# Batch 1's loads in another order: v from SyncE behind a VectorE write, weights and q, k ahead of the weighing on GpSimd

## The chip, the core and the metric

The kernel runs on one core of a Trainium2 chip. The time is the device time of one execution in microseconds (us), and the median of several executions counts. The profile is of one execution; its span runs from the first to the last instruction, and all positions below are microseconds from the span's start.

## What is computed

Attention with a forget gate over 8 batches of 8 heads (576 tokens, head size 64), and then a two-layer feed-forward with an exact gelu over the 4608 tokens of width 512 (hidden width 2048):

```
scores = q @ k.T / 8
cum    = cumsum(log(clip(f, 1e-4, 1)), axis=-1)
scores = where(causal, -1e9, scores + cum[:, :, :, None] - cum[:, :, None, :])
attn   = softmax(scores)
x      = (attn @ v) laid out as [batch * tokens, heads * 64]
h      = x @ w_in
out    = (0.5 * h * (1 + erf(h / sqrt(2)))) @ w_out
```

All inputs and the output are float32 in memory.

## The kernel before, in words

The gate never enters the scores. The kernel computes a running product of f (`wT`, per token and head) and multiplies v by it: row j of v, and an extra column of ones, are scaled ("weighed") by token j's factor into the bf16 tile `vw`. Attention is then exp(scores) times `vw`, divided by the extra column. `weigh_v` (lines 283 to 295) does this for two heads at a time, on GpSimd for all batches but a part of batch 0: one product of 128x640 (line 288) and one cast of the factors (line 295). `vw` has one buffer and `v_sb`, the float32 tile that v is loaded into, has one too; so batch 1's v cannot be loaded before batch 0's last weighing (line 764) has read it.

Tokens lie on the 128 partitions in five blocks (the last overlaps the fourth and uses 64 partitions). Of a batch, two heads form a pair; for each pair TensorE computes four tiles of scores (line 319), ScalarE takes the exponential (line 329), GpSimd masks the diagonals (line 331), TensorE multiplies by `vw` (`attend`, line 350), and VectorE divides (lines 363, 364). The result is transposed into `xT`, and the feed-forward follows: `gemm1` (line 405), gelu on ScalarE (line 425), `gemm2` in several forms (lines 449, 509, 545, 569).

The schedule is written by hand: the order of the program text is the order of each engine's queue, and an engine that waits holds up all that is queued behind it. Work of neighbouring batches is interleaved on TensorE, so that the feed-forward of batch b fills the gaps of the attention of batch b+1.

Batches 0 and 1 have q and k loaded into stacked tiles (`load_qk_tokens`, lines 98 to 125): the tile called "q" holds q and k of heads 0 to 3, the tile called "k" those of heads 4 to 7, so a row of the profile that reads `k<-in_k_dram` is k of heads 4 to 7. TensorE transposes them, a pair of heads at a time (`transposes_first`, lines 217 to 241, matmuls of line 226). From batch 2 on, SyncE (SP) transposes q and k by DMA (line 255), and VectorE sorts them (line 269).

Transfers that convert float32 to bf16 are issued from GpSimd: q and k, w_in in quarters (line 184), w_out in quarters of 512 rows (line 188). v is not converted. `load_v` (lines 129 to 137) issues five transfers, one for each block of tokens, of the heads it is given, on the engine it is given, SP if none is named. Batches 0 and 1 have v issued from GpSimd, the later ones from SP.

Around the change, the parts of the text are these:

- `first_attention` (line 706) is batch 0's attention. At its lines 756 to 774 GpSimd's queue gets, in this order: w_in's quarters 0 to 2 between the weighings of batch 0, q and k of batch 1 of heads 0 to 3 (two heads at a time), the last weighing (line 764), a small write to `v_sb` (line 770), v of batch 1 for heads 0 to 3, w_in's quarter 3, q and k of heads 4 to 7 in one piece, v for heads 4 to 7.
- The loop of lines 952 to 981 is the rest of `gemm1` of a batch. At its step 7 of batch 0 (lines 965 to 972) GpSimd gets the weighing of pair 0 of batch 1, a quarter of w_out, the weighing of pair 1, another quarter of w_out, and q and k of batch 2; TensorE gets the transposes of pair 0 of batch 1.
- `second_attention` (line 882) is batch 1's attention. Its order on TensorE: the scores of pair 0 (`tiles(0, 0)`, `tiles(0, 2)`) between the transposes of pairs 1 and 2 and the held blocks 10 to 12 of batch 0's `gemm1`, the first scores of pair 1, block 13, and then `run(0)`, which is `attend` of pair 0 and is the first to read batch 1's `vw`. Blocks 12 to 15 read w_in's last quarter. The other weighings (pairs 2 and 3) and the masks of pairs 1 to 3 lie on GpSimd behind the two of step 7, in the order in which TensorE needs them. SP gets batch 2's transposes (lines 925, 926), GpSimd a small read of batch 2's k as a gate (line 931, instruction of line 595) and w_out's other half behind it.

Of the kernel before, what the change touches and what calls it, by code (L numbers as in the profile page):

```python
# [54 lines left out]
def kernel(  # L55
# [10 lines left out]
    nc = tc.nc  # L66
# [31 lines left out]
    def load_qk_tokens(b, h0=0, h1=H):  # L98

        if b >= B:  # L100
            return
        stacked = b < 2
        if b not in qk_of:
            qk_of[b] = [
                qk_pool.tile(
                    [P, H // 2, J0 * D] if stacked else [PT, H, JT * D],
                    BF16,
                    tag=n,
                    name=f"{n}{b}",
                )  # L110
                for n in "qk"
            ]
        for which, src in enumerate((q, k)):
            if stacked:
                half, g0 = divmod(h0, H // 2)
                g1 = h1 - half * (H // 2)
                dst = qk_of[b][half][which * D : (which + 1) * D, g0:g1, :]
            else:
                dst = qk_of[b][which][:, h0:h1, :]
            nc.gpsimd.dma_start(  # L120
                dst,
                src[b, h0:h1].rearrange(
                    "h (p j) d -> p h (j d)", j=J0 if stacked else JT
                ),
            )
# [3 lines left out]
    def load_v(b, h0=0, h1=H, eng=nc.sync, ns=range(NBLK)):  # L129
        if b >= B:  # L130
            return
        for n in ns:
            p0 = D if n == NBLK - 1 else 0
            eng.dma_start(  # L134
                v_sb[p0:P, h0:h1, n, :],
                v[b, h0:h1, K0[n] + p0 : K0[n] + P].rearrange("h p d -> p h d"),
            )
# [79 lines left out]
    def transposes_first(b, i, pool, tag, both=(0, 1), parts=1):  # L217

        half, g = divmod(2 * i, H // 2)
        src = qk_of[b][half]  # L220
        pss = {w: pool.tile([P, J0, D], BF16, tag=tag, name="ps_f") for w in both}
        for j in range(J0):
            for which in both:
                rows = slice(which * D, (which + 1) * D)
                for h in range(2):
                    nc.tensor.transpose(
                        pss[which][h * D : (h + 1) * D, j, :],
                        src[rows, g + h, j * D : (j + 1) * D],
                        ident_bf[rows, rows],
                    )  # L230

        for which in both:
            dst = (qT, kT)[which][i].rearrange("d (p j) -> d p j", j=J0)
            ps = pss[which].rearrange("d j p -> d p j")
            copies = [nc.vector.tensor_copy] * parts
            if b == i == 0:
                copies = [nc.vector.tensor_copy, nc.scalar.copy]
            n = D // len(copies)
            for at, copy in enumerate(copies):
                part = slice(at * n, (at + 1) * n)  # L240
                copy(dst[:, part], ps[:, part])
# [41 lines left out]
    def weigh_v(b, i, eng=nc.gpsimd, n0=0, n1=NBLK):  # L283

        hs = slice(2 * i, 2 * i + 2)
        bh = b * H + 2 * i
        w = wT[:, n0:n1, bh : bh + 2].rearrange("p n h -> p h n")
        eng.tensor_tensor(  # L288
            vw(b)[:, hs, n0:n1, 0:D],
            v_sb[:, hs, n0:n1, :],  # L290
            w.unsqueeze(3).to_broadcast([P, 2, n1 - n0, D]),
            Alu.mult,
        )
        if b:
            eng.tensor_copy(vw(b)[:, hs, :, D], w)
# [410 lines left out]
    def first_attention():  # L706

        most = NBLK - 1

        def transposes(i, which, parts=1):  # L710
            transposes_first(0, i, m_psum, "m", (which,), parts)

        warm_up(9)
        for which in range(2):
            transposes_first(0, 0, o_psum, "o", (which,))
        nc.vector.tensor_tensor_scan(
            decay[:, S - 2 :: -1],
            f_sb[:, S - 1 : 0 : -1],
            none[:, 0 : S - 1],
            2.0**80,  # L720
            Alu.mult,
            Alu.add,
        )
        warm_up(2, 2 * P)
        scores_a(0)
        scores_b(0)
        transposes(1, 0)
        transposes(1, 1, 2)
        psw = o_psum.tile([P, NBLK, BH], FP32, tag="o", name="psw")
        for n in range(NBLK):  # L730
            nc.tensor.transpose(
                psw[:, n, :], decay[:, K0[n] : K0[n] + P], ident_fp[:BH, :BH]
            )
        idle = o_psum.tile([P, TC], FP32, tag="o", name="ps_w")

        def keep():
            nc.tensor.matmul(idle, warm[:, 0:P], warm, start=True, stop=True)

        scores_a(1)
        nc.vector.tensor_copy(wT[:, 0:4, :], psw[:, 0:4, :])  # L740
        nc.vector.tensor_copy(wT[D:P, 4, :], psw[D:P, 4, :])
        nc.vector.tensor_copy(
            vw(0)[:, :, :, D], wT[:, :, 0:H].rearrange("p n h -> p h n")
        )
        transposes(2, 0)
        scores_b(1)
        transposes(2, 1)
        scores_c(0, 1)
        transposes(3, 0)
        scores_a(2)  # L750
        transposes(3, 1)
        keep()
        scores_b(2)
        weigh_v(0, 0, nc.vector, 0, most)
        weigh_v(0, 1, nc.vector, 0, most)
        load_w_in(0)
        load_v(0, 0, 8, nc.gpsimd, [most])
        load_w_in(1)
        weigh_v(0, 2, n1=most)
        weigh_v(0, 3, n1=most)  # L760
        load_w_in(2)
        load_qk_tokens(1, 0, 2)
        load_qk_tokens(1, 2, 4)
        nc.gpsimd.tensor_tensor(
            vw(0)[:, :, most, 0:D],
            v_sb[:, :, most, :],
            wT[:, most, 0:H].unsqueeze(2).to_broadcast([P, H, D]),
            Alu.mult,
        )
        nc.gpsimd.memset(v_sb[:, :, 0, 0:1], 0.0)  # L770
        load_v(1, 0, 4, nc.gpsimd)
        load_w_in(3)
        load_qk_tokens(1, 4, 8)
        load_v(1, 4, 8, nc.gpsimd)
        scores_a(3)
        keep()
        attend_0(0, 0)
        attend_0(0, 1)
        scores_c(2, 3)
        scores_b(3)  # L780
        attend_0(1, 0)
        attend_0(1, 1)
        to_xT_0(0, nc.scalar.copy)
        attend_0(2, 0)
        to_xT_0(1, nc.scalar.copy)
        attend_0(2, 1)
        scores_t(0)
        scores_t(2)
        attend_0(3, 0)
        to_xT_0(2, nc.vector.tensor_copy)  # L790
        attend_0(3, 1)

        three = range(HP - 1)
        pss = [gemm1(0, 0, three)]
        scores_t4()
        pss += [gemm1(0, 1, three, spare())]
        to_xT_0(3, nc.vector.tensor_copy)
        pss += [gemm1(0, 2, three, spare())]
        for ffb in range(3):
            gemm1(0, ffb, (HP - 1,), pss[ffb])  # L800
        gemm1(0, 3)
# [143 lines left out]
    for b in range(B):  # L945
        if b == 0:
            first_attention()
        elif b == 1:
            second_attention()
        else:  # L950
            attention(b)
        for ffb in range(4 if b < 2 else 5, n_ff):
            if b == 0 and ffb in HELD:
                continue
            aside = ffb in (7, 8) if b > 1 else b == 1 and ffb % 4 < 2
            gemm1(b, ffb, ps=spare() if aside else None)
            if b == 1 and ffb % 2 == 0:
                at = HELD[(ffb - 4) // 2]
                gelu(0, at, h_of[at])
            if b == 0:  # L960
                if ffb == 4:
                    attend_tail()
                if ffb == 5:
                    tail_0()
                if ffb == 7:
                    weigh_v(1, 0)
                    load_w_out(0)
                    weigh_v(1, 1)
                    load_w_out(1)
                    load_qk_tokens(2)  # L970
                if ffb == 7:
                    transposes_first(1, 0, o_psum, "o")
            elif b + 1 < B:
                first, gap = (5, 3) if b == 1 else (1, 4)
                at, late = divmod(ffb - first, gap)
                if late == 0:
                    untangle(b + 1, at)
                if late == gap - 2 and (b > 1 or at < 2):
                    weigh_v(b + 1, at)
                if ffb == (9 if b == 1 else 14):  # L980
                    load_qk_tokens(b + 2)
# [34 lines left out]
```

## Time and profile before

| | |
|---|---|
| median of 3 runs | 334.8 us |
| lowest, highest | 334.04, 337.23 us |
| the profiled execution's own time | 335.03 us |
| its span | 333.1 us |
| granted TensorE clock, mean | 0.999 |
| DMA packets | 94980, 44.18 MB, mean 133 GB/s |

The span is shorter than the execution's time, which also holds what lies around the instructions. In the profile PE is TensorE, PEld its weight loads, DVE is VectorE, ACT ScalarE, POOL GpSimd, SP SyncE; L350 is line 350. A row of a timeline gives start and length in us, the engine, the line, the operation, the tile written and the tiles read, shapes, the count, and in brackets the idle time of that engine just before and what ended it. DMA queue q0 carries what GpSimd issues, q1 what SP issues; a row of a queue gives packets, megabytes, and the time of the packets as a share of 16 engines' time in that stretch (packets overlap within an engine, so it can pass 100%).

In the stretch from 7 to 50 us the DMA engines are nearly always busy, at some 200 GB/s.

### The profile page before, as it was taken

The numbers are of one execution on the slowest core, as the hardware profiler recorded it, in microseconds if no ns is written. First come the engines' busy times: TensorE is split into PE (matmuls) and PEld (weight loads), VectorE is DVE, ScalarE is ACT, GpSimd is POOL, SyncE is SP. The second block draws the span as 40 slices with busy tenths as digits, with TensorE's granted clock in tenths as the row PEclk, the third lists the DMA queues.
The fourth block names the chain that finished last, engine by engine and source line by source line (L and its number), as shares of the span: only waits on it lengthen the run. The fifth ranks groups of instructions, "written<-read, shape, count | busy, mean of one in ns | idle before, by whom it ended". The sixth has DMA issues, their size and how long they took to land.

```text
span 333.1 us, 8058 instructions
## 1 busy us (share of the span) xinstructions
PE 324.5 (97%) x3287; PEld 169.5 (51%) x3287; DVE 184.3 (55%) x427; ACT 205.8 (62%) x296; POOL 135.4 (41%) x262
## 2 busy tenths in 40 slices
PE   7999799999999999999999999999999999999995
PEld 3765455445554466445644565455544654444443
DVE  6853556664549764894589447954795450010011
ACT  4886686974526786578737892788278836405600
POOL 8997873048337044704471344434432410000000
PEclk9999999999999999999999999999999999999999
DMA  7999999979999799489939896879700420020022
GB/s 122 195 193 195 214 195 146 184 150 180 203 199 175 119 213 159 96 138 184 202 106 140 169 194 130 124 146 212 155 0 3 100 76 33 0 92 36 0 51 76
DMA packets 94980, 44.18 MB, mean 133 GB/s; under 512 B 74208, under 2 KB 89824, under 8 KB 94944
## 3 DMA queue, kind: packets, MB, share of 16 engines
q1 hardware_dynamic: 77760, 27.16, 41.4%
q0 software_dynamic: 16784, 15.99, 30.5%
q8 instruction: 25, 0.41, 0.5%
q10 hardware_dynamic: 400, 0.52, 0.4%
q14 instruction: 11, 0.09, 0.1%
HBM read 36.85 MB, written 9.44 MB: 139 GB/s over the span
## 4 chain that ended last, share of the span: by engine, by line
PE 87%; POOL 6%; DMA 5%; issue 0%; ACT 0%; DVE 0%; POOLq 0%
PE ps L405 34%; PE ps L509 27%; PE ps L449 8%; PE o L350 8%; PE s L319 6%; DMA w_in_sb<-in_moe_w_in_dram 3%; DMA k<-in_k_dram 3%; POOL v_sb L169 2%; PE ps L569 1%; POOL k L120 1%; PE ps L545 1%; POOL q L120 1%; POOL vw L288 1%; POOL v_sb L134 1%; POOL w_in_sb L184 1%
## 5 line engine op out<-in xcount | busy, mean ns | idle before, releaser
L425 ACT ACTIVATE g<-ps 128x512 bf16<-128x512 f32 x138 | 78.5, 602 | 79.4 <-PE ps L405 78.8
L405 PE MATMUL ps<-xT,w_in_sb 128*128 128x512 bf16 x512 | 114.0, 379 | 0.1
L509 PE MATMUL ps<-w_out_sb,g 64*128 64x512 bf16 (+1 forms) x711 | 108.1, 377 | 0.0
L329 ACT ACTIVATE e<-s 128x896 bf16<-128x896 f32 x112 | 87.6, 836 | 22.2 <-PE s L319 19.7
L405 PEld LDWEIGHTS <-w_in_sb 128*128 128x128 bf16 x576 | 55.3, 98 | 66.5 <-issue 2.6
L331 POOL TENSOR_SCALAR_AFFINE_SELECT e<-e 128x256 bf16<-128x256 bf16 (+1 forms) x135 | 49.1, 383 | 88.6 <-ACT e L329 88.2
L509 PEld LDWEIGHTS <-g 64*128 64x128 bf16 (+1 forms) x711 | 39.4, 95 | 34.7 <-issue 4.2
L288 POOL TENSOR_TENSOR vw<-v_sb,wT 128x640 bf16<-128x640 f32 (+1 forms) x30 | 38.4, 1279 | 25.5 <-DMA v_sb<-in_v_dram 15.4
L269 DVE COPY kT<-tk 64x288 bf16<-64x288 bf16 x96 | 42.9, 447 | 2.6 <-DMA tk<-k 1.0
L269 DVE COPY qT<-tq 64x288 bf16<-64x288 bf16 x96 | 39.9, 415 | 4.0 <-DMA tq<-q 2.6
L517 DVE COPY ot<-ps 128x512 f32<-128x512 f32 x20 | 13.8, 692 | 46.9 <-PE ps L509 46.9
L319 PE MATMUL s<-qT,kT 64*128 64x256 bf16 (+1 forms) x336 | 37.1, 276 | 0.5 <-ACT e L329 0.4
L350 PEld LDWEIGHTS <-e 128*128 128x128 bf16 x840 | 30.3, 98 | 7.9 <-POOL e L331 2.5
L458 DVE COPY ot<-ps 128x512 f32<-128x512 f32 (+2 forms) x9 | 5.7, 633 | 49.6 <-PE ps L449 49.6
L350 PE MATMUL o<-vw,e 128*128 128x65 bf16 x840 | 32.3, 194 | 0.0
L364 DVE TENSOR_TENSOR x<-o,r 128x320 bf16<-128x320 f32 x56 | 27.5, 492 | 3.2 <-DMA xT<-x 1.3
L449 PE MATMUL ps<-w_out_sb,g 128*128 128x512 bf16 (+2 forms) x144 | 28.0, 355 | 0.0
L319 PEld LDWEIGHTS <-kT 64*128 64x128 bf16 x336 | 16.8, 94 | 19.2 <-issue 4.5
L449 PEld LDWEIGHTS <-g 128*128 128x128 bf16 x144 | 13.5, 98 | 14.5
L529 DVE TENSOR_TENSOR ot<-ot,ps 128x512 f32<-128x512 f32 x22 | 15.1, 685 | 1.1
L363 DVE RECIPROCAL r<-o 128x5 f32<-128x5 f32 x56 | 10.5, 188 | 9.1 <-PE o L350 9.1
L405 PE MATMUL ps<-tails,w_in_sb 128*128 128x512 bf16 x64 | 14.3, 377 | 0.0
(89 smaller groups left out, 187.9 us busy)
## 6 DMA issues: line engine op xcount, KB each, us to landing
out_dram<-ot SPq DMA_DIRECT2D x32, 256.0 KB, 2.4
v_sb<-in_v_dram SPq DMA_DIRECT2D x24, 256.0 KB, 4.8
q<-in_q_dram POOLq DMA_DIRECT2D x6, 576.0 KB, 6.5
k<-in_k_dram POOLq DMA_DIRECT2D x6, 576.0 KB, 8.7
v_sb<-in_v_dram POOLq DMA_DIRECT2D x17, 128.0 KB, 5.3
w_in_sb<-in_moe_w_in_dram POOLq DMA_DIRECT2D x4, 512.0 KB, 7.0
w_out_sb<-in_moe_w_out_dram POOLq DMA_DIRECT2D x4, 512.0 KB, 8.2
v_sb<-in_v_dram SPq DMA_DIRECT2D x6, 128.0 KB, 4.6
```

Source lines behind the costliest of these rows:

```text
L269: nc.vector.tensor_copy(rows[:, odd], src[odd * D : (odd + 1) * D, 2 * i + h].rearrange("d j p -> d p j"),)
L288: eng.tensor_tensor(vw(b)[:, hs, n0:n1, 0:D], v_sb[:, hs, n0:n1, :], w.unsqueeze(3).to_broadcast([P, 2, n1 - n0, D]), Alu.mult,)
L319: nc.tensor.matmul(to, *ab, start=half < 0, stop=half == 1 or not masked)
L329: nc.scalar.activation(et[:, :, z:c], st[:, :, z:c], Act.Exp, scale=scale)
L331: nc.gpsimd.affine_select(out=et[:, :, c0 + z : c0 + P], in_=et[:, :, c0 + z : c0 + P], compare_op=Alu.is_ge, fill=0.0, base=z, pattern=[[ ...
L350: nc.tensor.matmul(o[:, m, :], e_of[b, i, t][:, h, c : c + P], vw_of[b][:, 2 * i + h, n, :], start=(n == 0), stop=(n == m),)
L364: nc.vector.tensor_tensor(x_of[b, i][:, :, h, :], o[:, :, 0:D], r.unsqueeze(2).to_broadcast([P, NBLK, D]), Alu.mult,)
L405: nc.tensor.matmul(ps, w_in_sb[:, kt, ffb * P : (ffb + 1) * P], src[:, kt, 0:TC], start=(kt == 0), stop=(kt == n_dm - 1),)
L425: nc.scalar.activation(g_of[c][ffb], ps, Act.Gelu)
L449: nc.tensor.matmul(pss[ts][:, c0:c1], g_of[c][kt][:, ts * P : (ts + 1) * P], w_out_sb[:, kt, c0:c1], start=(kt == 0), stop=(kt == n_ff - 1),)
L509: nc.tensor.matmul(banks[r], g_of[c][kt][rows, ts * P : (ts + 1) * P], w_out_sb[rows, kt, :], start=kt == (steps.index("r") if r else 0), ...
L529: nc.vector.tensor_tensor(ot, ot, bank, Alu.add)
```

## The change

```diff
@@ first_attention
-        nc.gpsimd.memset(v_sb[:, :, 0, 0:1], 0.0)
-        load_v(1, 0, 4, nc.gpsimd)
         load_w_in(3)
-        load_qk_tokens(1, 4, 8)
-        load_v(1, 4, 8, nc.gpsimd)
+        load_qk_tokens(1, 4, 6)
+        load_qk_tokens(1, 6, 8)
         scores_a(3)
@@ the loop over gemm1, batch 0
                 if ffb == 7:
-                    weigh_v(1, 0)
+                    transposes_first(1, 0, o_psum, "o")
+                    nc.vector.memset(v_sb[:, :, 0, 0:1], 0.0)
+                    load_v(1, 0, 4)
+                    load_v(1, 4, 8)
                     load_w_out(0)
-                    weigh_v(1, 1)
                     load_w_out(1)
                     load_qk_tokens(2)
-                if ffb == 7:
-                    transposes_first(1, 0, o_psum, "o")
+                    weigh_v(1, 0)
+                    weigh_v(1, 1)
```

Batch 1's ten transfers of v are issued from SP, in place of GpSimd. The small write to `v_sb`, which the first of them waits for, is VectorE's, in place of GpSimd's, and stands on VectorE behind the copies of the transposes of pair 0. On GpSimd, w_in's last quarter and q and k of heads 4 to 7, now two heads at a time, come directly behind the last weighing of batch 0; then follow half of w_out and q and k of batch 2, and only then the weighing of pairs 0 and 1, which were between these before. On SP, v stands ahead of the transposes of batch 2. TensorE's, ScalarE's and (but for the write) VectorE's instructions and their order stay as they are.

## The prediction, made before the changed kernel was run

> **What bounds the kernel now.** I read the page's engine shares first, then the chain that ended last around the change (17 to 41 us), then the timelines of TensorE and GpSimd there, then the DMA rows of single stretches, because the change moves transfers and nothing else.
>
> ```profile
> PE 324.5 (97%) x3287; PEld 169.5 (51%) x3287; DVE 184.3 (55%) x427; ACT 205.8 (62%) x296; POOL 135.4 (41%) x262
> ```
>
> TensorE is the bound: of the 333.1 us span it is idle for 8.6. Of these, 1.3 lie before its first matmul and 4.1 after its last one (which ends at 329.08), so some 3.2 us are all that any change of order can win. The chain shows the largest piece of them:
>
> ```profile
> 17.54 9.08 DMA w_in_sb<-in_moe_w_in_dram
> 26.90 1.37 POOL v_sb L134 x2
> 28.27 0.75 POOL w_in_sb L184
> 29.64 8.40 DMA k<-in_k_dram
> 38.08 0.47 PE ps_f L226 x34
> ```
>
> Read it upwards: TensorE's transposes of heads 4 and 5 (L226) start at 38.08 because k of heads 4 to 7 (the tile "k") landed at 38.04; it was issued at 29.64 because GpSimd had stood still until w_in's third quarter landed at 26.62. In the timelines (start, length, instruction, idle time before it) TensorE loses 1.35 us there, and the first weighted attention of batch 1 (L350) follows at 39.82:
>
> ```profile
> 38.08 0.47 PE L226 MATMUL ps_f<-key_of,k 64*64 64x64 bf16 x34 [1.35 <-DMA k<-in_k_dram]
> 39.82 1.11 PE L350 MATMUL o<-vw,e 128*128 128x65 bf16 x30
> ```
> ```profile
> 20.68 1.12 POOL L764 TENSOR_TENSOR vw<-v_sb,wT 128x512 bf16<-128x512 f32 x1
> 22.14 2.32 POOL L134 DMA_DIRECT2D v_sb<-in_v_dram  x3 [0.30 <-POOL v_sb L770]
> 26.90 1.37 POOL L134 DMA_DIRECT2D v_sb<-in_v_dram  x2 [2.43 <-DMA w_in_sb<-in_moe_w_in_dram]
> 29.64 0.63 POOL L120 DMA_DIRECT2D k<-in_k_dram  x1
> 33.87 1.33 POOL L288 TENSOR_TENSOR vw<-v_sb,wT 128x640 bf16<-128x640 f32 x1
> 35.10 0.27 POOL L295 CAST vw<-wT 128x10 bf16<-128x10 f32 x1
> ```
>
> GpSimd's queue holds eight transfers: w_in, four of q and k and three of v went out from 17.54 on, and the ninth waited for the first. The weighing of heads 0 and 1 ends at 35.37, so today vw is 4.45 us early for L350. The DMA rows of five stretches carry the rest: 60 to 62 us, where GpSimd's w_out (q0) and SP's transposes (q1) run together; w_out alone (40 to 42); q and k of batch 2 alone (45 to 48); v from SP alone (64 to 66); v from GpSimd (28 to 29):
>
> ```profile
> q0 software_dynamic: 304, 0.31, 91.2%
> q1 hardware_dynamic: 306, 0.08, 29.6%
> ```
> ```profile
> q0 software_dynamic: 390, 0.38, 121.3%
> ```
> ```profile
> q0 software_dynamic: 780, 0.59, 128.5%
> ```
> ```profile
> q1 hardware_dynamic: 2019, 0.50, 129.4%
> ```
> ```profile
> q0 software_dynamic: 85, 0.21, 89.7%
> ```
>
> Each line gives packets and MB. Together the two queues take turns one packet for one packet (304 to 306), though q0's packets have 1024 bytes and q1's 256. From SP, v goes in packets of 250 bytes (0.50 MB in 2019); from GpSimd it went in packets of kilobytes (0.21 MB in 85, completions included). On 16 engines the rows give, per engine: w_out 82 ns a packet alone (2 us x 16 / 390), q and k of batch 2 61.5 ns, v from SP 16 ns, and a pair of w_out and a 256-byte packet 105 ns (2 us x 16 / 304).
>
> **The change, part by part.**
>
> *w_in's last quarter, q and k ahead of v on GpSimd.* They go out from 21.8 us, where L764 ends: w_in, q and k of heads 4 and 5 fill the eight, q and k of heads 6 and 7 follow from 26.9. In the queue the packets of q and k of heads 0 to 3 give way to the next transfer near 27.2 (the rate per slice rises there as v's large packets begin). From there, per engine: w_in 32 packets x 82 ns = 2.6, q and k 32 x 89 = 2.8 (375 packets in 33.5 to 35.5 us make 85 to 89). Heads 4 and 5 are in at about 31.5 plus 1 of landing, 4 us before TensorE asks at 36.5. The wait of 1.36 goes, and TensorE stands at L350 at 39.82 - 1.36 = 38.5.
>
> *Half of w_out, q and k of batch 2 ahead of weighing.* Six issues of 0.6 to 0.8 us more: GpSimd is through at about 31.3, before it can have any v, so the issues themselves cost nothing. w_out begins in the queue at 27.2 + 2.6 + 2.8 = 32.6 and has 64 packets per engine (1024 of 1024 bytes on 16), then batch 2's q and k 96 (1536 of 768 bytes). Alone they are 5.2 + 5.9 us; w_out's first need (L545, 45.49) and the transposes of batch 2 (48.68) stay covered, and these are needed by TensorE only at 67.9.
>
> *v on SP behind the VectorE write.* The write stands behind the copies of the first transposes (30.49 + 0.75 = 31.24) and takes 0.18 as on GpSimd (L770), in time in which VectorE is idle until 32.65. SP has nothing before 48.68, so nothing waits behind its v but the transposes of batch 2. v's first packet comes at about 32.4: an estimate, issue at 31.5 and 0.6 to 1.2 from issue to first packet. So v meets w_out and batch 2's q and k, all in the other queue. v of heads 0 to 3 is 4 x 576 rows of 256 bytes, 144 per engine, one for each packet of q0: 64 beside w_out at 105 ns = 6.7 us, to 39.3; the other 80 beside q and k of batch 2. No row shows that pair: from below it is 61.5 + 16 = 77 ns, from above 61.5 + 28; I take 61.5 + 23 = 84.5, since 23 is what the small packet adds beside w_out, the nearest row. 80 x 84.5 ns = 6.8, to 46.1. From last packet to landing 0.5 to 2.0 us (k of heads 4 to 7: packets gone by some 36.5, landed 38.04); I take 1.0: 47.1.
>
> *What waits.* GpSimd stands at weighing from 31.3 to 47.1, and the five masks of pair 1 and the other weighings are queued behind it. The weighing and its cast take 1.50 (33.87 to 35.37): vw is there at 48.6, L350 starts 8.8 later than today. What follows keeps its distance: the second weighing (1.5) and the masks are done some 4 us after L350 starts, as now; v of heads 4 to 7 runs nearly alone by then (some 130 x 16 ns = 2.1 us) and is in by 50.5, before the third weighing asks at about 52. SP's transposes of batch 2 come behind v near 50, where they are now (48.68), and w_out's second half, behind GpSimd's gate (51.36), moves with the stall as its reader does (L569, 67.90): nothing.
>
> *The clock.* TensorE is idle for 10 us. At the end of the trace, after the last matmul at 329.08, the granted clock (column before the DMA share) reads
>
> ```profile
> 331.00:332.00 1.00, 0.00 (x0) 0.00 (x0) 0.00 (x0) 0.00 (x0) 0.00 (x0) 1.00 0.06 14
> 332.00:333.00 1.00, 0.00 (x0) 0.00 (x0) 0.00 (x0) 0.00 (x0) 0.00 (x0) 0.60 0.03 8
> ```
>
> so it halves about 3.1 us into idleness; at the start nine 512-column matmuls took 3.71 us, 0.41 each, against 0.22 later (31 in 6.85 from 54.48). After the stall some 3.3 us run at half speed: +1.6 (0 if the array were kept awake, 3.3 if it took two such stretches).
>
> *Sum.* The profiled execution took 335.03 us, 1.9 of it around the span and 0.23 above the median of 334.8. 335.0 + 8.8 + 1.6 = 345.4 us.
>
> *A rule beside the rows.* The Trainium skill's "DMA: Bandwidth & Descriptors", section "SWDGE vs HWDGE vs iDMA", has a DMA engine change queues only at packet boundaries, a packet being preferably up to 4096 bytes. By that v would move 16 rows a turn against four of w_out: an estimate from the page's figure is 9 turns of 0.26 + 0.33 us, v in by 38.7, vw at 40.2, and a sum of 335.4. The trace shows GpSimd's v in packets of that kind, but SP's in single rows, and I hold by it.
>
> **The rivals.** (1) *Fair shares by time or bytes* (10%): v of heads 0 to 3 is 144 x 16 ns = 2.3 us alone, 4.6 at half of the engines' time: in at 38.0, vw at 39.5 against 39.82 today: 334.7 us. For it speaks only that the 304 to 306 is seen with SP's transposes and not with its plain loads. (2) *v is hidden, not slower* (7%): if SP's packets pass the other queue, v lands at 32.4 + 2.3 + 1.0 = 35.7, vw is there at 37.2 before TensorE asks at 38.5, and only the wait goes: 335.0 - 1.4 = 333.6. It decides at a landing of 38.3 (39.82 - 1.50): earlier than that the kernel is not slower. Against it: q1's packets thin out beside q0 in the trace, from 1000 to 153 a us. (3) *Two to four of SP's packets in a turn* (15%): with two, 72 turns, 64 x 114 + 8 x 93 ns = 8.0, landing 41.4, vw 42.9: +3.1, and 4.4 idle, so +1.3 of clock: 339.4. (4) *The forecast* (68%).
>
> **How the numbers follow.** The forecast's own range: landing 0.5 to 2.0 and the pair 77 to 89.5 ns give -1.1 to +1.4, the clock -1.6 to +1.7, w_out's start -1 to +1: 342 to 349. To leave out no more than 2 in 10 the range takes in (3) and the upper side of (1): 336.0 to 349.0. A measurement tells about 1% (3.35 us) from no change. Slower by more: the forecast and (3) less a little, 0.81. Within: (1), (2) and the rest of (3), less 0.02: 0.17. Faster by more needs all 3.2 us of TensorE's idle time and more: 0.02, out of (2).
>
> **What would show it.** Right: no wait of L226 for k; L350 starting near 48.6 behind some 10 us of idle TensorE; GpSimd's L288 waiting for v_sb from 31 to 47; SP's v issued from 31.5; packet counts of q0 and q1 equal between 33 and 44; a granted clock below 1 near 45. Wrong: v in by 39, which falls if SP's loads take more than one packet a turn.

## The result, and the profile after

The kernel after takes 348.99 us (median of 6 runs, 347.92 to 349.82), against 334.45 us for the kernel before beside it (6 runs, 334.04 to 337.23): a ratio of 1.0415, with a 95% interval of 1.0379 to 1.0451. It is 4% slower. The profiled execution took 348.06 us, with a span of 346.2 (before: 335.03 and 333.1), so 13.1 us of span are to be found.

The engine shares and the granted clock in 40 slices:

```profile
PE 328.7 (95%) x3287; PEld 171.5 (50%) x3287; DVE 187.0 (54%) x428; ACT 206.3 (60%) x296; POOL 129.6 (37%) x253
...
PEclk9699968999999999999999999999999999999999
```

TensorE has the same 3287 instructions and is busy 4.2 us longer: the clock dips twice, near 10 to 18 us and near 45 to 55 us. The second dip is the effect of the change. The first lies ahead of anything that the change touches, and it seems to have cost nothing in the end (experiment e4, below, has none, and its stall ends at the same place). TensorE's timeline around the stall:

```profile
38.70 0.48 PE L226 MATMUL ps_f<-key_of,k 64*64 64x64 bf16 x36
...
39.57 1.04 PE L405 MATMUL ps<-xT,w_in_sb 128*128 128x512 bf16 x4
50.95 1.81 PE L350 MATMUL o<-vw,e 128*128 128x65 bf16 x30 [10.34 <-POOL vw L295]
...
53.45 1.89 PE L405 MATMUL ps<-xT,w_in_sb 128*128 128x512 bf16 x4
...
56.15 1.04 PE L405 MATMUL ps<-xT,w_in_sb 128*128 128x512 bf16 x4
```

The wait for k of heads 4 to 7 is gone: L226 runs its 36 matmuls in one piece, with no idle time before it. Instead TensorE stands for 10.34 us before the first weighted attention, and then runs at half speed for a while: four matmuls of L405 take 1.89 us at 53.45 and 1.04 us at 56.15. What it waits for is read from GpSimd's timeline and from SP's:

```profile
32.31 0.78 POOL L120 DMA_DIRECT2D k<-in_k_dram  x1 [1.74 <-PE ps_f L226]
49.45 1.27 POOL L288 TENSOR_TENSOR vw<-v_sb,wT 128x640 bf16<-128x640 f32 x1 [16.37 <-DMA v_sb<-in_v_dram]
50.68 0.22 POOL L295 CAST vw<-wT 128x10 bf16<-128x10 f32 x1
```
```profile
33.47 15.88 SPq L134 DMA_DIRECT2D v_sb<-in_v_dram  x10
```

GpSimd has issued its last transfer at 33.1 and then waits 16.37 us for v. The chain that ended last gives the order of the steps (start, length, what):

```profile
33.42 0.04 DVE v_sb L965
...
35.66 13.63 DMA v_sb<-in_v_dram
...
49.45 1.27 POOL vw L288
50.73 0.18 POOL vw L295
...
50.95 1.81 PE o L350 x30
```

The last of the first five transfers of v was issued at 35.66 and landed at 49.29. Between that issue and the weighing nothing else lies on the path. The DMA rows of three stretches, 35 to 37, 41 to 43, and 47 to 48 us, tell why it took 13.63 us:

```profile
q0 software_dynamic: 399, 0.40, 121.4%
```
```profile
q0 software_dynamic: 374, 0.28, 88.8%
q1 hardware_dynamic: 374, 0.09, 36.0%
```
```profile
q1 hardware_dynamic: 939, 0.23, 106.0%
q0 software_dynamic: 27, 0.02, 11.9%
```

Until 37 us only GpSimd's queue moves; then the two queues go one packet for one packet, 374 to 374 (39 to 41 and 43 to 45 us: 375 to 375 and 376 to 375); and when GpSimd's queue runs out, near 46, SP's rate is five times as high: 939 a us against 187. The stretches of 39 to 45, 45 to 51 and 51 to 55.2 us (busy time of TensorE, its weight loads, VectorE, ScalarE, GpSimd; granted clock, DMA share, GB/s) show the clock:

```profile
39.00:45.00 6.00, 1.61 (x36) 0.76 (x21) 2.11 (x3) 2.01 (x3) 0.00 (x0) 1.00 1.27 192
45.00:51.00 6.00, 0.05 (x2) 0.05 (x2) 0.00 (x0) 0.00 (x0) 1.54 (x3) 0.51 0.92 181
51.00:55.20 4.20, 4.20 (x38) 2.16 (x37) 1.37 (x4) 1.51 (x2) 2.94 (x7) 0.50 1.05 173
```

The DMA engines are busy all through the stall: TensorE's data is moved row by row beside data that nobody needs yet.

Sum, by how far TensorE's same instructions are shifted against before: +0.62 at L226 (+2.27 from the early dip, -1.36 for the wait for k, the rest in smaller pauses); +11.13 at L350; +13.0 at 55.3, where the clock is whole again; +13.2 at the last matmul.

### The profile page after: what moved, and what is told of

The parts are those of the page before. It is cut to its first block, busy times and chain, and to the rows that moved or that the text cites. A ratio compares the mean times of both kernels' runs of the same rounds, so it can differ in the third digit from the quotient of the medians.

```text
span 346.2 us, 8070 instructions
## 1 busy us (share of the span) xinstructions
PE 328.7 (95%) x3287; PEld 171.5 (50%) x3287; DVE 187.0 (54%) x428; ACT 206.3 (60%) x296; POOL 129.6 (37%) x253
## 4 chain that ended last, share of the span: by engine, by line
PE 82%; DMA 10%; POOL 4%; issue 1%; DVE 1%; SPq 1%; ACT 0%; POOLq 0%
PE ps L405 32%; PE ps L509 26%; PE o L350 8%; PE ps L449 8%; PE s L319 6%; DMA v_sb<-in_v_dram 5%; DMA w_in_sb<-in_moe_w_in_dram 2%; DMA k<-in_k_dram 2%; POOL v_sb L169 2%; DMA xT<-x 1%; PE ps L569 1%; POOL k L120 1%; PE ps L545 1%; POOL q L120 1%; POOL vw L288 1%
## 5 line engine op out<-in xcount | busy, mean ns | idle before, releaser
L405 PE MATMUL ps<-xT,w_in_sb 128*128 128x512 bf16 x512 | 115.0, 381 | 0.2
L405 PEld LDWEIGHTS <-w_in_sb 128*128 128x128 bf16 x576 | 55.4, 98 | 67.4 <-issue 3.6
L331 POOL TENSOR_SCALAR_AFFINE_SELECT e<-e 128x256 bf16<-128x256 bf16 (+1 forms) x135 | 49.3, 383 | 104.6 <-ACT e L329 104.0
L350 PE MATMUL o<-vw,e 128*128 128x65 bf16 x840 | 33.0, 195 | 10.3 <-POOL vw L295 10.3
L269 DVE COPY qT<-tq 64x288 bf16<-64x288 bf16 x96 | 41.8, 436 | 1.4
L350 PEld LDWEIGHTS <-e 128*128 128x128 bf16 x840 | 31.0, 99 | 18.4 <-issue 12.3
L363 DVE RECIPROCAL r<-o 128x5 f32<-128x5 f32 x56 | 10.6, 188 | 19.8 <-PE o L350 19.7
L624 ACT ACTIVATE e<-s 128x1024 bf16<-128x1024 f32 (+1 forms) x13 | 12.4, 990 | 3.9 <-PE s L619 3.5
```

The source lines that it names most:

```text
L269: nc.vector.tensor_copy(rows[:, odd], src[odd * D : (odd + 1) * D, 2 * i + h].rearrange("d j p -> d p j"),)
L331: nc.gpsimd.affine_select(out=et[:, :, c0 + z : c0 + P], in_=et[:, :, c0 + z : c0 + P], compare_op=Alu.is_ge, fill=0.0, base=z, pattern=[[ ...
L350: nc.tensor.matmul(o[:, m, :], e_of[b, i, t][:, h, c : c + P], vw_of[b][:, 2 * i + h, n, :], start=(n == 0), stop=(n == m),)
L405: nc.tensor.matmul(ps, w_in_sb[:, kt, ffb * P : (ffb + 1) * P], src[:, kt, 0:TC], start=(kt == 0), stop=(kt == n_dm - 1),)
```

## The experiments

The theory: v is late because each 256-byte row that SP moves has to wait for one packet of GpSimd's queue, which the change has filled with w_out and batch 2's q and k. Its rivals: the new order on GpSimd or the VectorE write would cost as much without that (A); the late start of v, not the turns, sets its landing (B); half of the loss is the clock (C). And what became of the 1.36 us of the wait for k? Ratios are against runs of the kernel before on the same chip, whose median was 335.14 us beside e1 to e4, 334.65 beside e5 to e10 and 334.97 beside e11.

### e1: the new order, with v on GpSimd

```diff
 (kernel before, first_attention)
+        load_w_in(3)
+        load_qk_tokens(1, 4, 6)
+        load_qk_tokens(1, 6, 8)
         nc.gpsimd.memset(v_sb[:, :, 0, 0:1], 0.0)
         load_v(1, 0, 4, nc.gpsimd)
-        load_w_in(3)
-        load_qk_tokens(1, 4, 8)
         load_v(1, 4, 8, nc.gpsimd)
```

> The kernel before with only the order of GpSimd's first loads changed: w_in's last quarter and q and k of heads 4 to 7 (two heads at a time) ahead of v, v still from GpSimd, w_out where it was. Theory (v loses because it sits in SP's queue against a backlog in GpSimd's): v goes in its turn in packets of 4 KB, is in by some 36.5 us, vw by 38.0, TensorE's wait for k (1.36 us) is gone and nothing takes its place: about 333.6 us, 1.0 to 1.4 below the kernel before. Rival (v is late because of what was put ahead of it, whichever queue it is in): L350 waits from 38.5 to 41 or later and the time is 336 or more.

Measured: 338.74 us, ratio 1.0083 (1.0049 to 1.0118). The stall is gone: L226 starts at 37.52, L350 at 39.27 without a wait. The theory's time was missed; the rival's was met, but not by the wait at L350 that it named. TensorE's timeline, then GpSimd's and VectorE's:

```profile
43.98 0.23 PE L350 MATMUL o<-vw,e 128*128 128x65 bf16 x2 [0.36 <-POOL e L331]
44.93 1.32 PE L350 MATMUL o<-vw,e 128*128 128x65 bf16 x28 [0.71 <-POOL e L331]
...
74.26 0.37 PE L509 MATMUL ps<-w_out_sb,g 64*128 64x512 bf16 x1 [1.43 <-DVE ot L577]
```
```profile
55.67 0.18 POOL L595 CAST gate<-k 96x1 f32<-96x1 bf16 x1 [3.33 <-DMA k<-in_k_dram]
```
```profile
68.07 1.35 DVE L269 COPY qT<-tq 64x288 bf16<-64x288 bf16 x4 [1.42 <-DMA tq<-q]
...
73.52 0.69 DVE L577 TENSOR_TENSOR ot<-ot,ps 128x512 f32<-128x512 f32 x1
```

GpSimd weighs some 3.7 us later than before (37.57 against 33.87), so the masks of pair 1 (L331) come too late for pair 1's attention, 1.07 us. Batch 2's k is late too, as the gate (L595) shows, and with it SP's transposes. VectorE gets the last of them at 68.07, copies without a break until 73.5 and only then comes to L577, for which TensorE waits at 74 us, 1.8 us with the pause behind. The reader of w_out's second half (L569) starts at 68.86 without a wait, so that half, which also stands behind the gate, is not what is late. The order itself therefore costs 3.6 us (338.74 against 335.14), not 14.

### e2: the changed kernel, weighing where it was

```diff
 (kernel after, step 7)
                     load_v(1, 4, 8)
+                    weigh_v(1, 0)
                     load_w_out(0)
+                    weigh_v(1, 1)
                     load_w_out(1)
                     load_qk_tokens(2)
-                    weigh_v(1, 0)
-                    weigh_v(1, 1)
```

> The changed kernel with the weighings of pairs 0 and 1 back between w_out's quarters, so that GpSimd issues no w_out and no q, k of batch 2 until v is in. Theory (packets in turn with GpSimd's backlog): SP's v meets only the rest of q and k, lands near 37, L350 starts near 39, time 333.6 to 336. Rival (SP's loads behind the VectorE write are late by themselves): L350 still near 47 to 51, time 345 to 349.

Measured: ratio 1.0176 (1.0099 to 1.0254); four executions took 337.09, 339.58, 342.66 and 343.72 us, all above the 333.6 to 336 expected. The first is the profiled one; what the others lost is not known. v comes from SP behind the VectorE write, as in the changed kernel, but w_out's issue waits for the weighing, so GpSimd's queue is nearly empty while v moves. SP's timeline, the DMA rows of 34 to 36 us, and TensorE's timeline:

```profile
31.40 7.07 SPq L134 DMA_DIRECT2D v_sb<-in_v_dram  x10
```
```profile
q1 hardware_dynamic: 1382, 0.34, 76.8%
q0 software_dynamic: 5, 0.00, 1.4%
```
```profile
38.61 1.11 PE L350 MATMUL o<-vw,e 128*128 128x65 bf16 x30
```

1382 packets in 2 us against 374, and L350 starts at 38.61 with no wait, 12 us earlier than in the changed kernel. The backlog in GpSimd's queue is the cause of the stall; v on SP and the VectorE write alone stall nothing. That rules out rival A for the stall. What remains lost in this execution are masks (0.58 and 0.71 us at 44) and smaller pauses.

### e3: v in rows of 1 KB

```diff
 (kernel after, load_v)
-    v_sb = consts.tile([P, H, NBLK, D], FP32)
+    v_store = consts.tile([P, NBLK, H, D], FP32)
+    v_sb = v_store.rearrange("p n h d -> p h n d")
...
+            if b == 1:
+                flat = v[b].rearrange("h s d -> (h s d)")
+                at = (h0 * S + K0[n]) * D
+                eng.dma_start(
+                    v_store[p0:P, n, h0:h1, :].rearrange("p h d -> p (h d)"),
+                    flat[at : at + (P - p0) * (h1 - h0) * D].rearrange(
+                        "(p e) -> p e", p=P - p0
+                    ),
+                )
+                continue
```

Same bytes, a quarter of the rows; batch 1's v reaches other places than it should.

> The changed kernel with batch 1's v moved in rows of 1 KB in place of 256 bytes: same queue, same bytes, same ten transfers, a quarter of the packets (36 per engine for heads 0 to 3 in place of 144). Its values of v reach other places, so batch 1's output is not the reference's. Theory (one packet a turn): 36 turns of about 120 ns, v in by about 43, L350 near 44.5, stall some 5 us, time 338 to 341. Rival (the engines share by bytes or by time, or SP's queue only moves when GpSimd's is empty): L350 still at 49 to 51, time 346 to 349.

Measured: 341.57 us, ratio 1.0165 (1.0108 to 1.0222). The DMA rows of 36 to 40 us, and TensorE's timeline (L361 is L350 here):

```profile
q0 software_dynamic: 526, 0.50, 74.1%
q1 hardware_dynamic: 527, 0.48, 44.7%
```
```profile
43.63 1.81 PE L361 MATMUL o<-vw,e 128*128 128x65 bf16 x30 [4.69 <-POOL vw L306]
```

Again one for one, 526 to 527, though SP's packets have four times the bytes. The stall shrinks from 10.34 to 4.69 us, the time by 7.4 us, to half a microsecond above the 338 to 341 expected. Here the bytes are nearly equal as well, but in the changed kernel they were not (0.28 to 0.09 MB): only the count of packets fits both. This is the most direct support of the theory.

### e8: SP's loads nine microseconds earlier

```diff
 (kernel after: from step 7 to first_attention, behind to_xT_0(3, ...))
+        nc.vector.memset(v_sb[:, :, 0, 0:1], 0.0)
+        load_v(1, 0, 4)
+        load_v(1, 4, 8)
```

> The changed kernel with the VectorE write and SP's v issued near 23 us, where batch 0's last weighing ends, in place of 31.5 to 33.5. Theory (one packet a turn beside GpSimd's backlog): first packet near 26.5, then 144 turns beside w_in, q, k and w_out at 105 to 115 ns and a few beside batch 2's q and k: landing 43 to 44.5, L350 near 45 to 46, time 340 to 343: starting 9 us earlier wins 5 to 7. Rival (v is late by its late start alone): L350 9 us earlier, near 41 to 42, time 336 to 338.

Measured: 343.09 us, ratio 1.0258 (1.0240 to 1.0277). SP's timeline, the DMA rows of 34 to 36 us, TensorE's timeline:

```profile
22.86 21.80 SPq L134 DMA_DIRECT2D v_sb<-in_v_dram  x10
```
```profile
q0 software_dynamic: 311, 0.31, 91.0%
q1 hardware_dynamic: 308, 0.08, 29.6%
```
```profile
44.79 1.81 PE L350 MATMUL o<-vw,e 128*128 128x65 bf16 x30 [6.45 <-POOL vw L295]
```

L350 starts where the theory said (45 to 46) and not where rival B did (41 to 42). Issued 10.6 us earlier, v is there only 6.2 us earlier: at 308 in 2 us a turn takes 104 ns on each engine, and 144 of them 15 us. So the start matters, but it does not set the landing alone, and B fails as the main cause. Two profiles with the loads where the changed kernel has them say the same. In e4 SP's issue is at 31.52, 1.95 us earlier than in the changed kernel's profile, and L350 starts at 50.92 against 50.95; in e5 it is at 35.90, 2.43 us later, and GpSimd starts to weigh at 48.36 against 49.45.

### e4 and e5: TensorE kept awake in the stall

```diff
 (kernel after, second_attention)
         gemm1_hold(13)
+        warm_up(44)      (e5: 56)
         run(0)
```

These matmuls are extra work whose result is not used.

> The changed kernel with 44 idle matmuls of 512 columns (some 9.5 us at full clock) on TensorE between the held block 13 and L350, which fill the stall and change nothing that is computed. Theory (the stall costs its own length and the halved clock after it): L350 starts as before at 50 to 51, the clock stays at 1.00 after it, and 2.0 us are won: 346 to 347. Rival (the clock costs nothing here): no difference to the changed kernel, 348 to 349.

> As the kernel with 44 idle matmuls, but 56 of them (12.1 us), so that TensorE works until L350 can start. Theory (the halved clock after the stall is a cost of its own): L350 at 50.7 to 51.2, granted clock 1.00 in every run, span 343.5 to 344.5, time 345.5 to 346.2, so 2 to 3 below the changed kernel. Rival (what was lost after the stall is something else, such as masks or copies that come late): 347 to 348 as with 44.

Measured: e4 347.52 us, ratio 1.0329 (1.0268 to 1.0391). The 44 matmuls ended too soon, as TensorE's timeline and a stretch of the clock show:

```profile
38.49 9.66 PE L210 MATMUL ps_w<-warm 128*128 128x512 bf16 x44
50.92 1.11 PE L350 MATMUL o<-vw,e 128*128 128x65 bf16 x30 [2.77 <-POOL vw L295]
```
```profile
52.30:55.70 3.40, 3.40 (x53) 1.44 (x49) 1.31 (x5) 2.32 (x4) 3.05 (x7) 0.50 1.13 154
```

2.77 us of idleness were enough for 3.4 us at half speed, and these began 1.4 us after TensorE had work again. The time lies between what the theory (346 to 347) and the rival (348 to 349) said. e5 took 348.04 us, ratio 1.0400 (1.0353 to 1.0448), outside the 345.5 to 346.2 expected, in two groups: 349.94 and 350.29 us, and 346.13 and 345.91 us. The first is the profiled one:

```profile
42.87 12.25 PE L210 MATMUL ps_w<-warm 128*128 128x512 bf16 x55
54.96 1.11 PE L350 MATMUL o<-vw,e 128*128 128x65 bf16 x30
```

Here the array came up to full speed only near 20 us, and TensorE was some 4 us late before the stall; whether the 350.29 us began like that is not known. The matmuls run without a break up to L350, and L405 behind it takes 1.04 us: no halving. But vw was ready at 49.8, so here the extra matmuls themselves hold L350 up. The two faster executions had spans of 344.2 and 344.0 us, within the theory's 343.5 to 344.5, against 346.2: 2.0 to 2.2 us less. They were not profiled. With the 1.9 us by which the shift grows behind L350 in the changed kernel (11.13 to 13.0), the halved clock is worth some 2 us of the 13.1, about a sixth, and rival C fails.

### e6, e7, e9, e10, e11: where the 1.36 us go

These start from the kernel before and ask whether anything was to be won at the wait for k. e6 is e1 with w_out's first quarter issued ahead of both weighings:

```diff
 (e1, step 7)
+                    load_w_out(0)
                     weigh_v(1, 0)
-                    load_w_out(0)
                     weigh_v(1, 1)
```

> The first experiment (v from GpSimd behind w_in, q and k) with w_out's first quarter issued ahead of the weighing in place of behind it, so that the queue does not run dry from 38.5 to 40.5 us. Theory (what that experiment lost is a late queue: w_out's second half, which TensorE waits for at L509 near 74): that wait shrinks from 1.8 to below 0.5, L350 at 39.5 to 40, time 336.5 to 338. Rival (the loss is GpSimd's masks behind its issues, which stay as late): 338 to 340.

Measured: 336.03 us, ratio 1.0043 (1.0027 to 1.0059); less was lost than either expectation had it. TensorE waits 1.00 us for vw and 0.61 us for masks:

```profile
40.25 1.11 PE L350 MATMUL o<-vw,e 128*128 128x65 bf16 x30 [1.00 <-POOL vw L295]
...
45.27 1.32 PE L350 MATMUL o<-vw,e 128*128 128x65 bf16 x28 [0.61 <-POOL e L331]
```

e7 is the kernel before with the split of q and k alone:

```diff
-        load_qk_tokens(1, 4, 8)
+        load_qk_tokens(1, 4, 6)
+        load_qk_tokens(1, 6, 8)
```

> The kernel before with one thing changed: q and k of heads 4 to 7 loaded two heads at a time. Theory: the 1.36 us for k go, but GpSimd is through its issues 1.2 us later, so that the masks of pair 1 come up to 1 us late for L350's second use at 44: 334.2 to 335.5, within 0.4% of the kernel before. Rival (the wait for k is worth its full length): 333.4 to 333.8.

Measured: 336.24 us, ratio 1.0041 (1.0024 to 1.0057). TensorE's timeline and GpSimd's:

```profile
36.45 0.48 PE L226 MATMUL ps_f<-key_of,k 64*64 64x64 bf16 x36
...
43.25 1.32 PE L350 MATMUL o<-vw,e 128*128 128x65 bf16 x28 [0.64 <-POOL e L331]
...
72.70 0.37 PE L509 MATMUL ps<-w_out_sb,g 64*128 64x512 bf16 x1 [1.55 <-DVE ot L577]
```
```profile
54.45 0.18 POOL L595 CAST gate<-k 96x1 f32<-96x1 bf16 x1 [3.80 <-DMA k<-in_k_dram]
```

The time is above both expectations. The wait for k is gone, and L350 starts 1.63 us earlier than before; 0.64 us go back for masks at 43, and the rest and more at 72.7, where TensorE waits for VectorE as in e1: batch 2's k is late, the last transposes reach VectorE at 66.52 (1.50 us of waiting), and its copies end at 71.9 (69.7 in the kernel before). L569 reads w_out's second half from 67.18 on without a wait. What comes late stands behind GpSimd's queue, which has two more issues (some 1.2 us) and starts the first weighing 2.0 us later (35.91 against 33.87); that these issues are the whole cause is argued, not shown.

e9 adds the relief of GpSimd to e7, and e10 tries this relief alone, by giving only v of heads 4 to 7 to SP:

```diff
 (e9; e10 keeps load_qk_tokens(1, 4, 8) and has the last line alone)
+        load_qk_tokens(1, 4, 6)
+        load_qk_tokens(1, 6, 8)
-        load_qk_tokens(1, 4, 8)
-        load_v(1, 4, 8, nc.gpsimd)
+        load_v(1, 4, 8)
```

> The kernel before, with q and k of heads 4 to 7 loaded two heads at a time and v of heads 4 to 7 issued from SP; v of heads 0 to 3 stays on GpSimd. Theory (SP's 256-byte packets go one for one with GpSimd's, which matters only to what is due): v of heads 4 to 7 is needed first by the third weighing near 43 us, so it may crawl; 144 packets per engine at 85 ns from about 27 on have it in by about 40 to 42. GpSimd is rid of five issues (3.7 us), so the masks, w_out's second half and batch 2's q and k come earlier than in the kernel that was only split (336.2). 333.5 to 335.0 us, no wait for k at L226, no 3.8 us wait of the gate. Rival: the small packets add 23 ns to each of GpSimd's packets (some 64 of w_in, q and k: 1.5 us), so k lands late again or the masks are late all the same: 336 or more, with a wait at L226 or L350 or L331.

> The kernel before, with only v of heads 4 to 7 issued from SP. Theory: TensorE waits for k as before or some 0.5 to 1.5 us longer, as SP's packets go one for one with those of q and k (32 packets each delayed 23 ns = 0.7 us, w_in's last quarter the same); GpSimd is 3.7 us earlier at the weighings behind: 334.5 to 336 us. Rival: what GpSimd is rid of is worth more than the delay of k: below 334.

Measured: e9 336.24 us, ratio 1.0047 (1.0010 to 1.0084): the rival's time. The gate no longer waits, but w_in's last quarter is late; TensorE's timeline, and the DMA rows of 28 to 31 us:

```profile
37.30 1.04 PE L405 MATMUL ps<-xT,w_in_sb 128*128 128x512 bf16 x4 [1.62 <-DMA w_in_sb<-in_moe_w_in_dram]
38.27 0.82 PE L226 MATMUL ps_f<-key_of,k 64*64 64x64 bf16 x36
```
```profile
q0 software_dynamic: 196, 0.45, 60.3%
q1 hardware_dynamic: 1209, 0.30, 59.7%
```

Part of the loss is the clock again: it is halved from 38.49 to 41.91 (L226 takes 0.82 us for 0.48). Of the nine executions below 338 us, four with a mean clock of 0.995, the profiled one among them, took 336.17 to 337.15 us, and five with 0.999 or 1.000 took 334.56 to 335.48, about what the kernel before took (334.65). What the other three lost (338.66 to 339.55) is not known.

The DMA rows also bound the theory: here SP's packets pass six for one, at equal shares of time, while GpSimd's own v moves in packets of kilobytes. Whether such packets give way, or GpSimd's queue was short of work then, the rows do not tell; one for one is shown beside packets of some 0.75 to 1 KB (0.28 MB in 374, 0.31 MB in 311). e10 took 339.19 us, ratio 1.0115 (1.0064 to 1.0166), more than either theory said. In its profiled execution the array reached full speed only near 20 us, and TensorE was 4.7 us late by 17.5 us, before anything that the edit touches. Whether its other five executions began like that is not known, so e10 decides nothing.

e11 leaves all loads and changes TensorE's order alone, by putting pair 0's attention into the wait:

```diff
 (kernel before, second_attention)
         gemm1_hold(12, nc.scalar.copy)
+        run(0)
         transposes(2, o_psum, "o")
         tiles(1, 0)
         gemm1_hold(13)
-        run(0)
```

> The kernel before, with all loads as they were; only TensorE's order changes: the weighted attention of pair 0 of batch 1 (the 30 matmuls of L350, 1.1 us) stands ahead of the transposes of heads 4 and 5 in place of behind block 13. vw is ready at 35.4 and the last exponential of pair 0 at 36.5, so these matmuls can run from about 36.6 to 37.7 while k lands at 38.0. Theory (the wait for k is idle time of TensorE that only other TensorE work can win back; moving transfers only moves it): idle before L226 falls from 1.35 to about 0.3 to 0.4, and 333.6 to 334.3 us. Rival: the scores of pair 1 behind it then wait for the exponentials (L319 for L329, about 1 us), and the time is as before, 334.3 to 335.2.

Measured: 335.57 us, ratio 1.0034 (1.0001 to 1.0068): nothing won, and a little above both expectations, by a third mechanism.

```profile
37.42 1.15 PE L350 MATMUL o<-vw,e 128*128 128x65 bf16 x30
38.99 0.22 PE L226 MATMUL ps_f<-key_of,k 64*64 64x64 bf16 x2 [0.43 <-DVE r L363]
39.62 0.47 PE L226 MATMUL ps_f<-key_of,k 64*64 64x64 bf16 x34 [0.41 <-DVE x L364]
```

The transposes write the same PSUM tiles ("o") that the attention has just filled, and wait for VectorE's division of them, 0.84 us, with 0.16 and 0.28 us behind. None of the versions measured beats the kernel before.

## Why the prediction was right, and where its terms were off

The mechanism was right: the wait for k goes, v moves one row per packet of the other queue, TensorE stands for some 10 us and then runs at half clock for a while. The number was less so. The forecast was 345.4 us and the median is 348.99, at the very edge of the stated 336.0 to 349.0; three of the six executions lie above it. That the median falls inside is luck. The forecast's own upper margins (1.4 + 1.7 + 1.0) even add up to 349.5, where 349.0 was set.

- **The wait for k goes**: right. It was of no use, and not only because of the stall: e7 takes it away alone and ends 0.4% slower.
- **One SP packet for one of GpSimd's**: right. The pair was taken as 84.5 ns; 374 in 2 us on 16 engines make 85.6. 374 to 374 refutes the prediction's rivals (2) and (3), and together with e3, where four times the bytes change nothing in the count, rival (1). The rule that was weighed, of the Trainium skill's "DMA: Bandwidth & Descriptors", section "SWDGE vs HWDGE vs iDMA", gave an estimate of 335.4 us against 348.06 in the profiled execution. That queues change at packet boundaries fits these rows; the step that fails here is to fill SP's packet to 4096 bytes, since these were of 256.
- **The path from issue to first packet**: mis-sized. It was taken as 0.6 to 1.2 us and measured 3.64 (33.47 to 37.11); the issue itself came 2 us late in this execution (31.5 was said, e4 has 31.52). So v's first packet came at 37.11, not at 32.4, and w_out was nearly through by then: q0 moved 0.30 MB in 352 packets from 37 to 39 us, and 0.29 MB in 375 from 39 to 41, which is the 768 bytes a packet of batch 2's q and k. The term of 64 turns beside w_out (6.7 us) hardly took place. It cost little: with v starting later, fewer of its rows met the other queue, which ran out near 46. The sum as it was written had v start 4.7 us too early and take some 4 us too long, and that these two offset each other is luck.
- **The landing**: mis-sized. SP's counts are 306, 375, 374, 375 and 274 packets up to 46 us and 699 in the next one, so the 2304 rows of heads 0 to 3 (576 x 4) had begun by some 46.9, taken as 46.1; the last landed at 49.29. The lag was 2.4 us in place of 1.0; GpSimd's queue still had 27 packets between 47 and 48 us, so some DMA engines were behind the others, but the trace does not tell which. Weighing and cast took 1.46, with 1.50 said, so L350 starts 2.35 us later than the 48.6 predicted. This is the largest error in the time that was forecast.
- **The clock**: 1.9 us (shift 11.13 to 13.0) for 1.6. It stays halved from 45.08 to 55.32, 4.4 us of them with work.
- **The sum**: 345.4 + 2.35 + 0.3 = 348.05 us, against 348.06 in the profiled execution. The median lies 0.9 above that, for a reason that the profile does not hold: the spans of the six are 345.6 to 346.6, but three of them take 3.1 to 3.4 us around the span, where the profiled one takes 1.9.

Behind L350 TensorE waits no more than before: the masks, the second weighing, SP's transposes and w_out's second half are all there in time, as the prediction had it. They did not all keep their distance to L350: the second weighing, which the kernel before has done 2.3 us ahead of it (37.50 against 39.82), starts with it here (50.84).

## What to carry to other kernels

Before moving a load to another queue "to share the DMA engines", count packets and not bytes on both queues: here a tensor in 256-byte rows beside a long backlog of packets of 0.75 to 1 KB moved one row a turn until the backlog ended. Longer rows (e3) and a backlog that starts behind it (e2) both helped. A short wait on the critical path is only worth removing when the queue that serves it has slack behind it, which is read from that queue's next instructions (here masks, weighings and a load on which transposes depend). A stall of TensorE is dearer than its length: here the halved clock behind it cost some 2 us on top of 10.34.

## What the runs showed of the hardware that was not expected

- SP's first packet came 3.5 to 3.8 us after its issue in the seven profiles where GpSimd's queue was busy (3.64 after, 3.51 in e3, 3.63 in e4, 3.62 in e5, 3.83 in e8, 3.84 in e9, 3.74 in e10), and 1.15 us after it in e2, where that queue held little. The reason was not tried.
- The halved stretches lasted 10.24 us after (6.83 in its early dip), 6.83 us in e3 and in e8, and 3.41 us in e4 and e9: one, two or three times 3.41. The Trainium skill's "TensorE: Matmul & The Clock Gate", section "Part 1: The HAM clock gate (the "warmup" mystery)", describes a free-running window of 3413 ns that decides on the clock; these rows agree. A limit in plain idle time does not follow from it: 2.77 us were enough in e4 and 1.62 in e9. In the 3.41 us before the clock fell, TensorE was busy for 1.38 us in e4 (48.89 to 52.30) and 1.58 in e9 (35.08 to 38.49). Counted on from each profile's own changes of clock, stretches after which it did not fall have as little as 1.77 us in e1 (71.43 to 74.84) and 2.06 before (35.24 to 38.65). So here the share of work in a stretch of 3.41 us divides them, and not the length of one pause. The early dip after does not fit: 2.93 us of work came before it (7.54 to 10.95). No run tried the limit.
- In the profiled executions of e5 and e10 the array came up to full speed only at 20.2 and 20.7 us, against 4.1 to 6.6 in the other profiles. TensorE was 4.6 and 4.7 us late by then, before anything that the edits touch.
